# Block-sparse attention with a squared-ReLU layer on one core: key copies, v copies and order of the first chunk

## The chip, the cores and the metric

The kernel runs on one core of a Trainium2 chip. A core has a matrix engine (PE in the profile, with its weight loads as PEld), VectorE (DVE), ScalarE (ACT), GpSimd (POOL) and a queue engine (SP) that only starts transfers. Each engine works through its own list of instructions in order, and engines wait for each other by semaphores. The metric is the device time of one execution in microseconds (us); lower is better.

## The reference

```python
scores = scale * np.matmul(q, k.transpose(0, 1, 3, 2))
...
mask = np.abs(blk_i - blk_j) <= window
mask = mask | (blk_i == 0) | (blk_j == 0) | (blk_i == n_blocks - 1) | (blk_j == n_blocks - 1)
for qb in range(n_blocks):
    for kb in sampled_blocks[qb]:
        mask[qb * block:(qb + 1) * block, kb * block:(kb + 1) * block] = True
...
attn = attn / (np.sum(attn, axis=-1, keepdims=True) + 1e-09)
return np.matmul(attn, v).astype(np.float32)
...
h = np.maximum(x @ w_in, 0.0)
return (h * h @ w_out).astype(np.float32)
```

There are 4 batches of 8 heads, 768 positions and a head size of 64; 24 blocks of 32 positions. A block of queries attends to its neighbours, to the first and last block (the fixed blocks) and to 3 sampled blocks, whose indices are an input. The first and last block of queries attend to everything. The result, 3072 tokens of 512, goes through the dense layer 512 to 2048 to 512. All of it is float32.

## The kernel before

The queries of a batch make 6 tiles of 128 positions (4 blocks). Three tiles are a chunk; there are 8 chunks. The dense layer (`moe`) runs on one chunk while the attention of the next ones is woven into it. Before the first dense rows there is nothing to weave into, so the attention of chunk 0 runs alone, in a loop of its own near the end of the program.

**Units.** `Whole(b, pr)` handles the first and last block of queries for one pair of heads; `Half(b, t, u)` handles the other blocks of tile t for one half u of the heads (4 of 8). Both are generators: scores on PE, maxima on VectorE, exponentials on ScalarE (`exps`), transposes on PE (`turn`), copies out of PSUM (`copies`), the product with v on PE (`values`, tile `pv` or `pvg`), division by the sum on VectorE (`norm`). They yield after each step the number of steps to wait (`LAG_0`), and `Stream.step(now)` resumes them. `units(0)` gives the order: four Wholes, then six Halves, one every 5 steps (`STEP_0`). The order of the program is the order on each engine: it is written out by hand and nothing reorders it.

**Keys.** `load_keys` brings the keys of one half of the heads into a tile `kn` (24 blocks, 2 pairs of heads, 32 positions); POOL starts these two loads. For each tile of queries, `copy_keys` gathers on POOL what its 4 blocks need into `KG`: per half, the two fixed blocks for all four (`static_keys`, L297, 128x512) and then one copy per block and sample (L275, 128x64: two pairs of 32), whose source is addressed by a register. That is 24 small copies per tile (18 where a tile has only three blocks of its own). It yields after each block's three copies. Tiles 0 to 2 are copied before the loop; tiles 3 and 4 are put into `later` by the loop, and one yield of theirs is issued every second step (`KEYS_N`).

**v.** For each tile two tiles `V[k]` hold the rows of v that its blocks need: fixed rows, three window rows, three sampled rows. In chunk 0, tile 0's fixed rows come by DMA for one block and are copied by ScalarE to its other blocks (`copy_static`, L217); ScalarE also copies them for tiles 1 and 2, four copies of 64x1040, in steps 7 and on (`FIXED_0`). Tile 0's window rows come by DMA; those of tiles 1 and 2 are copied from `vn` with `copy_window` (L225, 32x260, twelve per tile and half): tile 1's first half and both halves of tile 2 on POOL, tile 1's second half on VectorE, one per step from step 22 (`MOVES_0`). The sampled rows come by DMA from SP (`load_sampled`, L323), one transfer per block and sample.

**Weights.** They arrive as 64-bit numbers. POOL starts the load of a block into `craw` (L782), ScalarE makes two parts of it (L798, L800), VectorE joins them (L809, L810), and the block of the first layer is split into a high and a low part: `WI` (ScalarE L816, POOL L817) or `wi` (ScalarE L842, POOL L845). `cut_next` moves this on by a stage. It is called five times before the loop, between POOL's key and v copies, then every 5 steps from step 35 (`CUT_0`), and inside the dense rows every 3 steps. The split of block 0 (L817) is issued at step 45, ahead of that step's load. The tiles `craw`, `wi` and others share one ring of 7 buffers.

**Dense rows.** `moe(0)` transposes the three tiles (`turn`), then for each of 16 weight blocks does `hidden` (12 matmuls into `ph`, L882: first with the high part, then the low part, then with the low part of x; then relu and square on ScalarE, L886 and L889) and, two blocks behind, `project` (L911). PE interleaves with this the scores of chunk 1.

Of the kernel before, what the change touches and what calls it, by code (L numbers as in the profile page):

```python
# [10 lines left out]
F32 = mybir.dt.float32  # L11
# [3 lines left out]
AF = mybir.ActivationFunctionType  # L15
# [8 lines left out]
BLK = 32  # L24
NBLK = S // BLK
NRAND = 3
P = 128
# [21 lines left out]
UC = 3  # L49
# [21 lines left out]
STEP_0 = 5  # L71
# [26 lines left out]
def tile_block_sparse_attention_moe(ctx: ExitStack, tc, kd, knd, qd, qgd, vd, vnd, samp, const, wcat, out):  # L98
# [9 lines left out]
    nc = tc.nc  # L108
    wide = wcat.dtype != F32

    one = ctx.enter_context(tc.tile_pool(name="one", bufs=1))
    rot = ctx.enter_context(tc.tile_pool(name="rot", bufs=2, reuse_waits="tile"))
# [12 lines left out]
    negative = one.tile([P, 1], F32, name="negative")  # L125
    nc.gpsimd.memset(negative, -SCALE)

    def indices():

        n = NBLK * NRAND  # L130
        si = rot.tile([1, 2 * n], I32, tag="r", name="si", bufs=2)
        nc.sync.dma_start(si, samp)
        rows = rot.tile([1, 6 * n], F32, tag="ct", name="rows", bufs=2)
        qb, s, m, d, keep, ne = (rows[:, i * n : (i + 1) * n] for i in range(6))
        nc.sync.dma_start(qb, const)
        nc.vector.tensor_copy(s, si.rearrange("p (r t) -> p r t", t=2)[:, :, 0])
        nc.vector.tensor_scalar(m, s, 0.5, None, op0=ALU.is_ge)
        nc.vector.scalar_tensor_tensor(m, s, NBLK - 1.5, m, op0=ALU.is_le, op1=ALU.mult)
        nc.vector.tensor_tensor(d, s, qb, op=ALU.subtract)
        nc.vector.tensor_tensor(d, d, d, op=ALU.mult)  # L140
        nc.vector.scalar_tensor_tensor(keep, d, 1.5, m, op0=ALU.is_ge, op1=ALU.mult)
        s3 = s.rearrange("p (b r) -> p b r", r=NRAND)
        k3 = keep.rearrange("p (b r) -> p b r", r=NRAND)
        ne = ne[:, :NBLK]
        for a, r in ((0, 1), (0, 2), (1, 2)):
            nc.vector.tensor_tensor(ne, s3[:, :, a], s3[:, :, r], op=ALU.not_equal)
            nc.vector.tensor_tensor(k3[:, :, r], k3[:, :, r], ne, op=ALU.mult)
        idx = one.tile([1, 2 * n], I32, name="idx")
        i4 = idx.rearrange("p (t i r) -> p t i r", i=2, r=NJ * NRAND)
        for i, x in enumerate((m, keep)):  # L150
            nc.vector.tensor_tensor(
                i4[:, :, i],
                x.rearrange("p (t r) -> p t r", t=NT),
                s.rearrange("p (t r) -> p t r", t=NT),
                op=ALU.mult,
            )
        return idx

    QG = one.tile([P, NPAIR, 2, BLK], F32, name="QG")
    V = {0: [one.tile([P, NJ, 2, HW // 2], F32, name=f"V{c}") for c in range(2)]}  # L160
    W1 = {f: one.tile([P, DM], F32, name=f"W1{f}") for f in SINGLE}
    KG = [one.tile([P, NJ, 2 + NRAND, NPAIR, BLK], F32, name=f"KG{i}") for i in range(2)]
# [4 lines left out]
    st = {}  # L167
# [3 lines left out]
    def load_whole(b, eng=nc.sync):  # L171

        eng.dma_start(QG.rearrange("p a b c -> p (a b c)"), qgd[b])

    def load_keys(b, u, eng=nc.sync):

        kn = rot.tile([P, NBLK, 2, BLK], F32, tag=f"kn{u}", name=f"kn{b}_{u}", bufs=1)
        eng.dma_start(kn.rearrange("p a b c -> p (a b c)"), knd[b, u])
        st["kn", b, u] = kn

    def values_of(k):

        return V[k if k < UC else 0]

# [3 lines left out]
    def halves(k, u):  # L188

        if k < UC:  # L190
            return slice(0, 2) if u == k // 2 else None
        return slice(u, u + 1)

    def columns(src, us):

        n = HW // 2
        return src[..., us.start * n : us.stop * n]

    def places(v, rows, js, us):

        return columns(v[rows, js].rearrange("p j u c -> p j (u c)"), us)

    def load_static(k, u, eng=nc.sync):
        us = halves(k, u)
        if us is None:
            return
        n = 1 if k == 0 else NJ
        src = columns(vd[order[k][0], V_STATIC * BLK :], us)
        src = src.unsqueeze(1).broadcast_to([2 * BLK, n, src.shape[-1]])
        eng.dma_start(places(values_of(k)[0], slice(0, 2 * BLK), slice(0, n), us), src)  # L210

    def copy_static(k, i, copy):

        us = slice(i, i + 1)
        src = places(V[0][0], slice(0, 2 * BLK), slice(0, 1), us)
        dst = places(V[k][0], slice(0, 2 * BLK), slice(1 if k == 0 else 0, NJ), us)
        copy(dst, src.broadcast_to(list(dst.shape)))  # L217

    def copy_window(k, i, j, n, copy):
# [4 lines left out]
        r = blk % NJ * BLK  # L224
        copy(V[k][1][(1 + n) * BLK : (2 + n) * BLK, j, i], st["vn", b, i][r : r + BLK, blk // NJ])  # L225

# [24 lines left out]
    def load_q(b, t, eng=nc.sync, own=None):  # L251
        q = (own or rot).tile([P, NJ, NPAIR, BLK], F32, tag="q", name=f"q{b}_{t}", bufs=1 if own else 2)
        n = NJ * NPAIR * BLK
        eng.dma_start(q.rearrange("p a b c -> p (a b c)"), qd[b, :, t * n : (t + 1) * n])
        st["q", b, t] = q
# [9 lines left out]
    def copy_keys(b, t, own=None):  # L265

        vals = sampled(t, 0, POOL)
        kg = keys_of(b, t, own)
        for u in range(2):
            if t < UC:  # L270
                static_keys(b, t, u, nc.gpsimd.tensor_copy)
            kn = st["kn", b, u]
            for j in sorted(groups(t)):
                for r in range(NRAND):
                    nc.gpsimd.tensor_copy(  # L275
                        kg[:, j, 2 + r, 2 * u : 2 * u + 2].unsqueeze(1), kn[:, bass.ds(vals[NRAND * j + r], 1)]
                    )
                yield

    later = []  # L280
# [12 lines left out]
    def static_keys(b, t, u, copy=nc.scalar.copy):  # L293

        src = st["kn", b, u][:, 0 : NBLK : NBLK - 1].rearrange("p i a c -> p i (a c)").unsqueeze(1)
        dst = st["kg", b, t][:, :, 0:2, 2 * u : 2 * u + 2].rearrange("p j i a c -> p j i (a c)")
        copy(dst, src.broadcast_to(list(dst.shape)))  # L297
# [13 lines left out]
    def load_sampled(k, u, eng, on):  # L311
        us = halves(k, u)
        if us is None:
            return
        b, t = order[k]
        VA, VB = values_of(k)
        vals = sampled(t, 1, on)
        v4 = columns(vd[b], us).rearrange("(a p) c -> p a c", p=BLK)
        for j in sorted(groups(t)):
            for r in range(NRAND):  # L320
                at = slice(0, BLK) if r == 2 else slice((2 + r) * BLK, (3 + r) * BLK)
                dst = places(VB if r == 2 else VA, at, slice(j, j + 1), us)
                eng.dma_start(dst, v4[:, bass.ds(vals[NRAND * j + r], 1)])  # L323
# [251 lines left out]
    class Whole:  # L575
# [32 lines left out]
        def scores(self):  # L608
# [4 lines left out]
            for g in range(NJ):  # L613
                kh, i = divmod(g, 2)
                for e in range(2):
                    r = slice(e * D, (e + 1) * D)
                    nc.tensor.matmul(  # L617
                        self.sg[e][g * BLK : (g + 1) * BLK, : self.n],
                        QG[r, pr, i],
                        kn[r, kh * NBLK // 2 : (kh + 1) * NBLK // 2, pr % 2, :],  # L620
# [98 lines left out]
    def units(c):  # L719

        halves = [Half(b, t, u) for b, t in order[c * UC : (c + 1) * UC] for u in range(2)]
        wholes = [] if c % 2 else [Whole(c // 2, pr) for pr in range(NPAIR)]
        if c == 0:
            return [(i * STEP_0, u) for i, u in enumerate(wholes + halves)]
        if c == 1:
            return [(i * STEP_1 + FIRST_1, u) for i, u in enumerate(halves)]
        at = begins(c - 1) - EARLY
        both = [(at + i * STEP, u) for i, u in enumerate(halves)]
        both += [(at + i * STEP + G_AT, u) for i, u in enumerate(wholes)]
        return sorted(both, key=lambda x: x[0])  # L730
# [250 lines left out]
    for k in range(1, UC):  # L981
        V[k] = [begin.tile([P, NJ, 2, HW // 2], F32, name=f"V{k}{c}") for c in range(2)]
    load_keys(0, 0, nc.gpsimd)
# [7 lines left out]
    load_q(0, 1)  # L991
    load_sampled(0, 0, nc.sync, SP)
    load_sampled(1, 0, nc.sync, SP)
    load_q(0, 2, own=begin)
    load_sampled(2, 1, nc.sync, SP)
    windows = {
        (k, u): [(copy_window, k, u, j, n) for j in range(NJ) for n in range(3)]
        for k in range(1, UC)
        for u in range(2)
    }  # L1000
    for k in range(2):
        deque(copy_keys(0, k), 0)
    for i in range(AHEAD + 1):
        if i == FIRST_LOADS:
            for f, *at in windows[1, 0]:
                f(*at, nc.gpsimd.tensor_copy)
        if i == SECOND_LOADS:
            deque(copy_keys(0, 2, begin), 0)
        if i == THIRD_LOADS:
            for f, *at in windows[2, 0] + windows[2, 1]:  # L1010
                f(*at, nc.gpsimd.tensor_copy)
        if i < AHEAD:
            cut_next()
    fixed = [(copy_static, k, i) for k in range(UC) for i in range(2)]
    moves = windows[1, 1]
    side = lambda name: ps_o.tile([P, 512], F32, tag="o", name=name)
    work = Stream()
    for at, u in units(0):
# [96 lines left out]
```

## Time and profile before

| | us |
|---|---|
| time, median of 3 runs | 748.9 (748.66 to 751.27) |
| the profiled execution | 750.76 |
| its span, first to last instruction | 749.0 |
| PE busy | 713.9 (95%) |
| DVE busy | 512.4 (68%) |
| ACT busy | 509.2 (68%) |
| POOL busy | 496.3 (66%) |

The page divides the span into 40 slices of 18.7 us and gives the busy share of each in tenths:

```profile
PE   4776999999999999999999999999999999999996
DVE  5985777757876775778877676678877677645432
ACT  4585786998876777579876777579876777622222
POOL 5997644237777466677867566667876566768783
```

A digit 9 is 90% or more. PE's first four slices, 75 us, are the attention of chunk 0 and the first dense rows; VectorE and POOL have their highest digits there. A timeline line reads: start, duration, engine, line of the program, operation, output<-inputs, shape, count, and in brackets the idle time before it with what ended it. Instructions on POOL overlap by some tens of nanoseconds, so the distance from start to start tells what one costs.

### The profile page before, as it was taken

How to read it: one execution, taken by the hardware profiler on the slowest of the kernel's cores; microseconds unless marked ns; L12 is line 12 of the kernel's file. 1: busy time of each engine (PE TensorE's matmuls, PEld its weight loads, DVE VectorE, ACT ScalarE, POOL GpSimd, SP SyncE). 2: the span in 40 equal slices, each digit the busy share in tenths (PEclk: the TensorE clock that was granted, in tenths of full speed). 3: DMA queues.
4: the chain of work that ended last, by engine and by line, in shares of the span. 5: the costliest groups of instructions: out<-in, count | busy, mean ns of one | idle time of the engine just before them, and what ended most of it. 6: DMA issues, size and time to landing. Idle time of an engine off the chain costs nothing.

```text
span 749.0 us, 25271 instructions
## 1 busy us (share of the span) xinstructions
PE 713.9 (95%) x9440; PEld 590.7 (79%) x9440; DVE 512.4 (68%) x992; ACT 509.2 (68%) x1121; POOL 496.3 (66%) x649
## 2 busy tenths in 40 slices
PE   4776999999999999999999999999999999999996
PEld 1565676668888888877888888877888888889895
DVE  5985777757876775778877676678877677645432
ACT  4585786998876777579876777579876777622222
POOL 5997644237777466677867566667876566768783
PEclk9998999999999999999999999999999999999999
DMA  8666789743443445544344344534344342101001
GB/s 273 199 173 196 230 238 311 202 126 98 121 104 101 113 107 164 157 99 122 97 125 111 80 132 131 182 92 142 86 129 108 86 132 52 33 2 42 1 1 43
DMA packets 84318, 92.49 MB, mean 123 GB/s; under 512 B 13507, under 2 KB 70596, under 8 KB 84196
## 3 DMA queue, kind: packets, MB, share of 16 engines
q1 hardware_dynamic: 78244, 68.03, 34.2%
q0 software_dynamic: 5664, 22.45, 9.3%
q8 instruction: 75, 1.23, 0.7%
q14 instruction: 47, 0.39, 0.2%
q10 hardware_dynamic: 288, 0.39, 0.1%
HBM read 84.53 MB, written 6.29 MB: 121 GB/s over the span
## 4 chain that ended last, share of the span: by engine, by line
PE 82%; POOL 4%; DVE 3%; issue 3%; DMA 3%; ACT 3%; POOLq 1%; SPq 0%; ACTq 0%
PE ph L882 34%; PE po L922 31%; PE s L401 6%; PE pv L496 5%; PE po L911 3%; POOL V L225 2%; POOL KG L275 2%; DMA KG<-in_k_dram 2%; PE pvg L685 1%; DMA V<-in_v_dram 1%; PE g L617 1%; DVE xl L872 1%; DVE WO L810 1%; ACT craw L800 0%; PE pv L511 0%
## 5 line engine op out<-in xcount | busy, mean ns | idle before, releaser
L446 ACT ACTIVATE pm<-p 32x256 f32<-32x256 f32 x528 | 219.3, 415 | 19.0 <-DVE p L421 11.3
L845 POOL TENSOR_TENSOR wo<-WO,wo 128x512 fp32r<-128x512 f32 x112 | 144.8, 1293 | 62.3 <-DVE wo L844 59.9
L882 PE MATMUL ph<-xh,wi 128*128 128x384 f32 x832 | 176.3, 348 | 7.4 <-POOL wi L845 5.3
L886 ACT ACTIVATE r<-ph 128x384 f32<-128x384 f32 x128 | 63.0, 492 | 168.3 <-PE ph L882 167.5
L845 POOL TENSOR_TENSOR wi<-W,wi 128x512 fp32r<-128x512 f32 x104 | 134.9, 1297 | 64.0 <-ACT wi L842 28.2
L922 PE MATMUL po<-wo,gh 128*128 128x512 f32 x672 | 176.0, 396 | 0.0
L901 POOL TENSOR_TENSOR gl<-gf,gh 128x384 fp32r<-128x384 f32 x112 | 113.8, 1016 | 85.3 <-DVE gf L898 70.3
L882 PEld LDWEIGHTS ph<-xh,wi 128*128 128x128 f32 x832 | 147.3, 188 | 28.5 <-issue 11.4
L898 DVE SCALAR_TENSOR_TENSOR gf<-ph,r 128x384 f32<-128x384 f32 x112 | 62.3, 556 | 146.8 <-ACT r L886 144.6
L922 PEld LDWEIGHTS po<-wo,gh 128*128 128x128 f32 x672 | 123.7, 188 | 24.4 <-issue 4.0
L922 PE MATMUL po<-wo,gl 128*128 128x512 f32 x336 | 98.5, 401 | 0.0
L882 PE MATMUL ph<-xl,wi 128*128 128x384 f32 x416 | 91.0, 341 | 0.0
L882 PEld LDWEIGHTS ph<-xl,wi 128*128 128x128 f32 x416 | 74.5, 189 | 2.0 <-issue 1.9
L922 PEld LDWEIGHTS po<-wo,gl 128*128 128x128 f32 x336 | 62.2, 189 | 16.9 <-issue 2.8
L844 DVE TENSOR_REDUCE wo<-WO 128x512 fp32r<-128x512 f32 x112 | 74.8, 668 | 0.0
L413 DVE TENSOR_REDUCE m<-s 128x2 f32<-128x512 f32 (+1 forms) x96 | 61.6, 683 | 12.2 <-PE s L401 12.0
L893 ACT ACTIVATE gh<-r 128x384 fp32r<-128x384 f32 x112 | 58.9, 526 | 10.0 <-ACT r L886 0.8
L844 DVE TENSOR_REDUCE wi<-W 128x512 fp32r<-128x512 f32 x91 | 61.0, 670 | 0.0
L401 PE MATMUL s<-KG,q 64*32 64x160 f32 x1408 | 48.2, 300 | 2.0 <-issue 1.1
L911 PE MATMUL po<-WO,gp 128*128 128x512 f32 x96 | 46.4, 618 | 0.0
L421 DVE TENSOR_TENSOR p<-s,m 128x512 f32<-128x512 f32 (+1 forms) x72 | 46.0, 679 | 0.0
L452 DVE STREAM_TRANSPOSE pT<-pm 128x1024 f32<-128x1024 f32 (+1 forms) x36 | 41.2, 1145 | 0.0
(95 smaller groups left out, 882.7 us busy)
## 6 DMA issues: line engine op xcount, KB each, us to landing
craw<-in_w_dram POOLq DMA_DIRECT2D x32, 512.0 KB, 5.2
V<-in_v_dram SPq DMA_DIRECT2D x462, 32.5 KB, 1.8
KG<-in_k_dram SPq DMA_DIRECT2D x198, 64.0 KB, 1.9
V<-in_v_dram SPq DMA_DIRECT2D x28, 390.0 KB, 4.1
q<-in_q_dram SPq DMA_DIRECT2D x24, 256.0 KB, 2.8
out_dram<-ot SPq DMA_DIRECT2D x22, 256.0 KB, 2.7
V<-in_v_dram SPq DMA_DIRECT2D x14, 292.5 KB, 4.2
vn<-in_vn_dram SPq DMA_DIRECT2D x5, 780.0 KB, 5.6
```

What stands on the lines that cost most here:

```text
L401: nc.tensor.matmul(self.sb[e][g * BLK : (g + 1) * BLK, i * NSLOT + a : i * NSLOT + z], q[r, j, pr, :], k, start=True, stop=True,)
L413: nc.vector.tensor_reduce(m[at, e], self.sb[e][at].rearrange("p (i c) -> p i c", i=2), axis=AX, op=ALU.max)
L446: nc.scalar.activation(p[a * BLK : (a + 1) * BLK, g], x[g * BLK : (g + 1) * BLK, :, a], AF.Exp, scale=SCALE)
L844: nc.vector.tensor_reduce(w[:, 0], src.unsqueeze(2), axis=AX, op=ALU.max)
L845: nc.gpsimd.tensor_tensor(w[:, 1], src, w[:, 0], op=ALU.subtract)
L882: nc.tensor.matmul(ph[:, :TOK], w, x, start=(i == 0), stop=(i == len(steps) - 1))
L886: nc.scalar.activation(r, ph[:, :TOK], AF.Relu)
L893: nc.scalar.activation(gh, r, AF.Square)
L898: nc.vector.scalar_tensor_tensor(gf, ph[:, :TOK], 0.0, r, op0=ALU.max, op1=ALU.mult)
L901: nc.gpsimd.tensor_tensor(gl, gf, gh, op=ALU.subtract)
L911: nc.tensor.matmul(acc[c][u], g[:, u * P : (u + 1) * P], WO[f], start=(f == 0), stop=(f == NF - 1))
L922: nc.tensor.matmul(acc[c][u], g[:, at], w[:, k], start=first, stop=(f == NF - 1 and g is gl))
```

## The change

Five things are changed, all for chunk 0.

- A one-element exponential is issued on ScalarE right after its operand `negative` is set.
- `kn` of both halves becomes one tile `KN` with the half as a dimension. `copy_keys` copies a sampled block for both halves in one instruction (128x128). For tile 0 it keeps the two passes, one per half. The other tiles have one pass, so half as many yields.
- The fixed rows of v for tiles 1 and 2 are loaded by DMA from SP, behind the sampled rows of tile 1; ScalarE's copies for these tiles are gone.
- The second half of tile 1's window rows is copied by POOL, ahead of tile 2's, and not by VectorE.
- `units(0)` puts the first Half behind the second Whole.

```diff
+    warm = one.tile([P, 1], F32, name="warm")
+    nc.scalar.activation(warm, negative, AF.Exp)
...
+    KN = one.tile([P, 2, NBLK, 2, BLK], F32, name="KN")
...
-        kn = rot.tile([P, NBLK, 2, BLK], F32, tag=f"kn{u}", name=f"kn{b}_{u}", bufs=1)
+        kn = KN[:, u]
...
-        for u in range(2):
+        for us in (slice(0, 1), slice(1, 2)) if t == 0 else (slice(0, 2),):
             if t < UC:
-                static_keys(b, t, u, nc.gpsimd.tensor_copy)
-            kn = st["kn", b, u]
+                for u in range(us.start, us.stop):
+                    static_keys(b, t, u, nc.gpsimd.tensor_copy)
             for j in sorted(groups(t)):
                 for r in range(NRAND):
-                    nc.gpsimd.tensor_copy(
-                        kg[:, j, 2 + r, 2 * u : 2 * u + 2].unsqueeze(1), kn[:, bass.ds(vals[NRAND * j + r], 1)]
-                    )
+                    to = kg[:, j, 2 + r].rearrange("p (u i) s -> p u (i s)", u=2)
+                    of = KN.rearrange("p u k i s -> p u k (i s)")
+                    nc.gpsimd.tensor_copy(to[:, us].unsqueeze(2), of[:, us, bass.ds(vals[NRAND * j + r], 1)])
                 yield
...
-            return [(i * STEP_0, u) for i, u in enumerate(wholes + halves)]
+            return [(i * STEP_0, u) for i, u in enumerate(wholes[:2] + halves[:1] + wholes[2:] + halves[1:])]
...
     load_sampled(1, 0, nc.sync, SP)
+    for k in range(1, UC):
+        load_static(k, k // 2)
     load_q(0, 2, own=begin)
...
         if i == THIRD_LOADS:
-            for f, *at in windows[2, 0] + windows[2, 1]:
+            for f, *at in windows[1, 1] + windows[2, 0] + windows[2, 1]:
                 f(*at, nc.gpsimd.tensor_copy)
...
-    fixed = [(copy_static, k, i) for k in range(UC) for i in range(2)]
-    moves = windows[1, 1]
+    fixed = [(copy_static, 0, i) for i in range(2)]
+    moves = []
```

## The prediction

> **What bounds the kernel now.** I read the head of the page first, then what the matrix engine waits for before 66 us and after 70 us, then the timelines of PE and POOL between 13 and 81 us.
>
> ```profile
> span 749.0 us, 25271 instructions
> PE ph L882 <- POOL wi L845: 5.3, 1, 5.3
> PE ph L882 <- DVE wi L844: 2.0, 2, 1.2
> ```
>
> The second line is the longest wait of PE between the attention of the first chunk and the dense rows; the third is the longest group of waits in all the time after 70 us. So PE sets the pace from 70 us on, and a gain must be made before that. The timeline of PE shows where:
>
> ```profile
> 51.19 1.38 PE L511 MATMUL pv<-V,pT 128*32 128x65 f32 x64 [0.92 <-ACT pT L485]
> 54.86 0.97 PE L882 MATMUL ph<-xh,WI 128*128 128x384 f32 x4 [0.82 <-ACT xh L871]
> 56.38 0.58 PE L401 MATMUL s<-KG,q 64*32 64x160 f32 x16
> 57.48 0.96 PE L882 MATMUL ph<-xh,WI 128*128 128x384 f32 x4 [0.51 <-POOL WI L817]
> 65.16 1.65 PE L882 MATMUL ph<-xh,wi 128*128 128x384 f32 x4 [5.32 <-POOL wi L845]
> 80.42 1.12 PE L511 MATMUL pv<-V,pT 128*32 128x65 f32 x64
> ```
>
> PE waits twice for POOL: 0.51 us for the low part of the first weight block (L817), then 5.32 us for that of the second (L845). POOL itself is never idle in between; it works through a queue:
>
> ```profile
> 13.90 1.65 POOL L275 COPY KG<-kn 128x64 f32 x9
> 15.49 0.61 POOL L297 COPY KG<-kn 128x512 f32<-128x512 f32 x1
> 16.05 2.18 POOL L275 COPY KG<-kn 128x64 f32 x12
> 20.85 1.05 POOL L782 DMA_DIRECT2D craw<-in_w_dram  x2
> 27.91 0.61 POOL L297 COPY KG<-kn 128x512 f32<-128x512 f32 x1
> 33.85 0.54 POOL L782 DMA_DIRECT2D craw<-in_w_dram  x1
> 34.44 12.16 POOL L225 COPY V<-vn 32x260 f32<-32x260 f32 x24
> 47.11 5.39 POOL L275 COPY KG<-kn 128x64 f32 x18
> 56.17 1.25 POOL L817 TENSOR_TENSOR WI<-ct,WI 128x512 fp32r<-128x512 f32 x1
> 57.38 0.58 POOL L782 DMA_DIRECT2D craw<-in_w_dram  x1
> 63.82 1.28 POOL L845 TENSOR_TENSOR wi<-W,wi 128x512 fp32r<-128x512 f32 x1
> ```
>
> Both waits end when POOL reaches an instruction that stands behind key copies. **POOL's queue is the bound of the first 65 us**, so the sum is made on it.
>
> **The change on POOL, step by step.** A merged key copy (128x128) is not in this trace. Nine copies of 64 elements fill 13.90 to 15.49, 0.177 us each; one of 512, read in eight runs of 64, fills 15.49 to 16.05, 0.56 us. So a further run of 64 costs (0.56-0.177)/7 = 0.054, and a merged copy 0.231 us. The bounds are 0.18 (a second run for nothing) and 0.355 (two old copies); I take 0.231, because the copy of 512 has the same runs.
>
> - Tile 1 ran from 15.49 to 20.85, 5.36 us: two fixed copies at 0.56 and 24 small ones. Now 2 x 0.56 + 12 x 0.231 = 3.89: -1.47.
> - Tile 2 ran from 27.91 to 33.85, 5.94 us. Now 3.89: -2.05; the copies that VectorE ran beside it are gone too.
> - Twelve copies of v move here, ahead of the 24 at 34.44. What one costs, and what VectorE's weight operations add, shows in the chain of work, copy by copy, with a row of VectorE's timeline below:
>
> ```profile
> 39.32 0.40 POOL V L225
> 39.78 0.79 POOL V L225
> 40.60 0.77 POOL V L225
> 39.59 0.70 DVE L809 SCALAR_TENSOR_TENSOR ct<-ct,craw 128x512 int32<-128x512 int32 x1
> ```
>
> Against a copy of 0.40, the two that start beside L809 and L810 take 0.79 and 0.77: such a pair costs POOL 0.76. Two pairs fell among the 24 copies (12.1 us), so one copy is (12.1-1.5)/24 = 0.44 and the twelve add +5.28.
> - Two more pairs fell on the 18 small copies at 47.11: 5.34-18 x 0.177 = 2.15. POOL now copies v until about 50 us and meets all four pairs there, at 0.76 each: -0.6.
> - Ahead of L817 stood 33 small copies of tiles 3 and 4. A tile now yields four times instead of eight, one yield for every second step, so tile 4 is through before the step that issues L817: 24 merged ones. 24 x 0.231 - 33 x 0.177: -0.3.
>
> L817 so starts 0.86 us later, at 57.03, ends near 58.3, and everything behind it is short: between 57.38 and 63.82 stood 15 small copies and three load issues. The copies are gone; the issues stay, 0.54 each. L845 starts at 58.3 + 1.6 = 59.9 instead of 63.82 and ends at 61.2. **PE's second block starts at 61.2 instead of 65.16: -3.9 us.**
>
> **What is late next.** ScalarE. Its timeline behind the first block:
>
> ```profile
> 59.17 0.49 ACT L886 ACTIVATE r<-ph 128x384 f32<-128x384 f32 x1 [3.85 <-PE ph L882]
> 64.70 1.54 ACT L460 ACTIVATE p<-s,m 128x256 f32<-128x256 f32 x4
> 68.13 0.49 ACT L886 ACTIVATE r<-ph 128x384 f32<-128x384 f32 x1 [1.89 <-PE ph L882]
> 73.66 0.61 ACT L816 CAST WI<-ct 128x512 fp32r<-128x512 f32 x1
> 75.20 0.49 ACT L886 ACTIVATE r<-ph 128x384 f32<-128x384 f32 x1 [0.93 <-PE ph L882]
> 77.37 0.56 ACT L485 COPY pT<-pt 128x512 f32<-128x512 f32 x1
> ```
>
> Take out its two waits for PE. From the first relu to the end of the exponentials it works 7.07 us (with a wait for VectorE), from the second relu to the end of L816 6.14, from the third to the end of the copy at 77.37 2.73: 15.94 in all. The first relu moves by the 0.86 of L817, to 60.03, so the copy ends at 75.97. The matmuls at 80.42 read it: they start at 76.0. PE would be there sooner (below), so ScalarE decides: **-4.4 us at 80.42**. From there PE has no gap longer than the waits shown, and I carry the 4.4 to the end.
>
> **The clock** belongs to it. Means by stretch (us; PE, PEld, DVE, ACT, POOL busy; PEclk; DMA share; GB/s):
>
> ```profile
> 10.00:12.00 2.00, 0.33 (x3) 0.31 (x3) 0.97 (x5) 1.99 (x4) 0.00 (x0) 1.00 1.02 332
> 12.00:14.00 2.00, 1.27 (x17) 0.54 (x19) 0.56 (x1) 2.00 (x4) 0.66 (x2) 0.75 1.04 330
> 64.00:66.00 2.00, 0.84 (x3) 0.84 (x4) 1.13 (x2) 2.00 (x6) 1.98 (x3) 0.55 0.73 188
> 70.00:72.00 2.00, 2.00 (x5) 0.72 (x3) 1.38 (x2) 0.46 (x2) 0.00 (x0) 0.74 0.87 342
> ```
>
> After the idle 5.32 us the granted clock is half from about 64.2 (a mean of 0.55 is 1.8 us of 2 at half) to 71.0 us (0.74 is 1.04 of 2), which costs PE (71.0-65.16)/2 = 2.9. From 65.16 to 80.42 PE thus has 15.26-2.9 = 12.3 us of work at full clock; from 61.2 it would be ready at 73.5, before ScalarE's 76.0. The new gap is shorter: the scores that end at 56.96 hang on the pv at 51.19, which then waits for POOL's last copy of v. POOL ends that at 33.85-3.5 (tiles 1, 2) + 0.6 + 36 x 0.44 + 4 x 0.76 = 49.8, so the scores end at 55.6 and PE is idle 2.7 us until 58.3. [...]
>
> **The parts that I cost at nothing**, since POOL covers them. VectorE loses twelve copies:
>
> ```profile
> L225 DVE COPY V<-vn x12: 285/292/695, 22.3 to 35.0; 32x260 f32<-32x260 f32 x12
> 30.00:35.00 5.00, 4.24 (x163) 3.37 (x153) 4.66 (x15) 2.42 (x6) 4.92 (x20) 1.00 0.62 173
> 9.65 1.28 ACT L641 ACT_TABLE_LOAD   x1 [9.65 <-DVE mg L634]
> ```
>
> VectorE is busy 4.66 us of 5 there, so at least 12 x 0.29 = 3.5 us less work there brings the attention's last pv from 51.19 towards 47.7, where POOL's 49.8 is later: about 2 us of this gain lie idle. The same holds for the table load (1.28 us off the first exponential) and for ScalarE's four copies of fixed blocks. The half tile moved up fills PE's wait for the second key half, but its pv must wait for the sampled rows of v that SP loads one by one, and whole tiles 2 and 3 queue behind it; the 2 us of cover hold that as well. If the cover were gone (POOL faster), each would count.
>
> The two DMAs go on SP's queue between the loads of tile 1 and q:
>
> ```profile
> 28.80 0.99 SPq L254 DMA_DIRECT2D q<-in_q_dram  x1
> 31.27 8.89 SPq L323 DMA_DIRECT2D V<-in_v_dram  x12
> V<-in_v_dram SPq DMA_DIRECT2D x1, 585.0 KB, 13.0
> ```
>
> Each carries 64 x 4 x 520 floats, 520 KB. Two issues at about half a us push the q load to 30 and the last sampled load of tile 2 from 40.2 to 41.2. The nearest landing is 13.0 us (585 KB, in the crowd at the start): lower bound of the harm 0, upper bound 28.8 + 13.0 = 41.8 for the pv of tile 1, which then runs 2 us late and is still covered. I take 0.
>
> **Sum.** 749.0 - 4.4 = 744.6 of span, 746.4 for the profiled execution of 750.76, which stands 1.9 above the median; against the median 748.9 that is **744.5 us**.
>
> **Rivals.**
> - *Half clock at the first block.* If PE's 2.7 us bring the gate down, the eight matmuls between 58.3 and the relu take twice their 1.7 us: the relu moves to 61.7, and 2.7 us are left: 746.2. For it: the fall at 12 to 14 us. Against: scores end only 2.7 us before.
> - *A merged copy costs as two (0.355).* POOL loses 48 x 0.124 = 6.0: L817 ends at 64.3, PE idles 8.7 us, the clock is surely half (+1.7). The matmuls at 80.42 start at 76.0 + 7.7 = 83.7: slower by 3.3, 752.2. The point at which nothing is left is 0.231 + 2.7/48 = 0.29 us a copy. Against it: the eight runs of the copy of 512.
> - *A merged copy costs 0.18.* POOL gains another 2.4; L817 ends at 55.9, hard behind the scores, with no gap: 742.1.
> - *The change does less than it says*: if the one key tile is tracked as a whole, the first copies and scores wait for the landing of its second half too. POOL's copies of the first half, now done before that, then stand in the queue like those of the second, which took 0.56 + 1.59 = 2.15 us up to 15.49; 4.4 - 2.15 are left: 746.7. Against it: at 54.86 PE reads one half of WI, while POOL has yet to write the other (only 57.48 waits for L817).
>
> **How the numbers follow.** Forecast 744.5: 0.48; half clock 0.20; two-for-one 0.13; 0.18 a copy 0.13; whole-tile wait 0.06. The range leaves out the two-for-one case and a little at the low end: 741.0 to 750.0. Half a per cent, 3.74 us (about what a measurement tells from no change), puts the border at 745.16, close above the forecast; I count 0.37 of its 0.48 below, with the 0.13 and 0.01 of the others: faster 0.51. Two-for-one lies at the upper border, half of it beyond: slower 0.09, with a little for a DMA that is late; same 0.40.
>
> **What would show it.** L275's copies on POOL at 0.23 apart; L817 starting near 57; no key copy between L817 and L845; L845 starting near 60; PE's wait there under 1 us; a granted clock of 1.0 from 58 to 71; PE then waiting for ScalarE's L485 before 76. L817 past 59, or the last pv waiting for V's DMA rather than POOL, would make me wrong.

## The result and the profile after

| | before | after |
|---|---|---|
| median of 7 runs each, us | 749.51 (746.57 to 753.12) | 745.61 (743.64 to 749.48) |
| ratio, 95% interval | | 0.9942 [0.9915, 0.9969] |
| profiled execution, us | 750.76 | 748.10 |
| its span, us | 749.0 | 746.3 |

The ratio is worth 4.3 us (the two medians are 3.9 apart), and the forecast was 4.4. The two profiled spans are only 2.7 us apart. In the first 66 us, PE's old waits for POOL are gone, and new ones stand elsewhere. This is the view of waits, after, from 0 to 66 us (who waited for whom: us in total, times, longest):

```profile
span 746.3 us, 25153 instructions
PE pv L515 <- issue: 5.8, 2, 4.6
PE pvg L689 <- issue: 3.1, 2, 1.8
POOL wi L849 <- ACT wi L846: 2.2, 1, 2.2
```

No line of PE waiting for POOL is left. Now POOL itself stands idle before L849 (L845 of before), because ScalarE brings its input late. Behind its start (6.3 us until the first keys land) the longest wait of PE is 4.6 us of "issue": no semaphore that the profile shows ended it. The timeline of POOL, after:

```profile
16.45 2.90 POOL L281 COPY KG<-KN 128x128 f32 x12
19.28 1.05 POOL L786 DMA_DIRECT2D craw<-in_w_dram  x2
30.65 16.69 POOL L229 COPY V<-vn 32x260 f32<-32x260 f32 x36
56.09 1.31 POOL L821 TENSOR_TENSOR WI<-ct,WI 128x512 fp32r<-128x512 f32 x1
57.32 1.62 POOL L786 DMA_DIRECT2D craw<-in_w_dram  x3
61.14 1.27 POOL L849 TENSOR_TENSOR wi<-W,wi 128x512 fp32r<-128x512 f32 x1 [2.21 <-ACT wi L846]
```

The merged copy takes (19.28 - 16.45)/12 = 0.236 us. L821 (L817 of before) starts at 56.09, and behind it stand only the three load issues. The timeline of PE, after:

```profile
34.16 0.87 PE L515 MATMUL pv<-V,pT 128*32 128x65 f32 x32
39.67 0.87 PE L515 MATMUL pv<-V,pT 128*32 128x65 f32 x16 [4.64 <-issue]
55.79 1.38 PE L515 MATMUL pv<-V,pT 128*32 128x65 f32 x64 [0.93 <-ACT pT L489]
64.15 1.57 PE L886 MATMUL ph<-xh,wi 128*128 128x384 f32 x8
75.34 1.98 PE L886 MATMUL ph<-xh,wi 128*128 128x384 f32 x8
77.55 1.58 PE L515 MATMUL pv<-V,pT 128*32 128x65 f32 x64 [0.23 <-issue]
```

PE stops in the middle of one product with v: 32 matmuls run, then nothing for 4.64 us, then the other 16 of the same group. Before, the same group stood at 34.17, and its break was 0.94 us, as the first of these two lines of PE's timeline before shows:

```profile
35.97 0.53 PE L511 MATMUL pv<-V,pT 128*32 128x65 f32 x15 [0.94 <-issue]
58.97 0.87 PE L882 MATMUL ph<-xh,wi 128*128 128x384 f32 x4
```

So the attention's last pv comes at 55.79, 4.6 us later than before (51.19). The second line concerns the second weight block. PE needs its high part first and then its low part, which L849 writes. Before, the four matmuls of the high part ran at 58.97, and the 65.16 of the prediction is the low part behind its wait. After, all eight run in one go from 64.15, and the low part, the fifth of them, starts near 64.9: only 0.3 us earlier. The pv of chunk 1 at 77.55 is 2.9 us earlier (80.42 before), and this reaches the end as 2.7 us of span. Between the low part and this pv lie 12.7 us instead of 15.3, mostly because the half clock that the prediction saw there from 64.2 to 71.0 no longer comes. What the stall leaves in the clock is in the windows of after (busy us of PE, PEld, DVE, ACT, POOL; granted clock; DMA share; GB/s):

```profile
36.00:40.00 4.00, 0.33 (x10) 0.33 (x12) 0.00 (x0) 0.37 (x1) 3.58 (x9) 0.89 0.80 250
40.00:44.00 4.00, 4.00 (x85) 3.16 (x79) 2.81 (x6) 2.12 (x5) 3.67 (x8) 0.50 0.42 97
44.00:48.00 4.00, 4.00 (x150) 3.46 (x136) 3.24 (x8) 2.93 (x7) 3.63 (x10) 0.75 0.84 251
```

From 36 to 40 PE works 0.33 us and VectorE nothing; only POOL works on. Then the granted clock is half: 0.89 is 0.9 us of 4 at half, 0.50 all of it, 0.75 is 2.0 us, together 6.9 us. It sets in at 39.1, while PE still stands. At the same place the DMA view shows slow landings. From 28 to 40 us, issues with KB each and median us to landing, first after, then before:

```profile
V<-in_v_dram SPq DMA_DIRECT2D x2, 520.0 KB, 7.1
craw<-in_w_dram POOLq DMA_DIRECT2D x1, 512.0 KB, 9.4
q<-in_q_dram SPq DMA_DIRECT2D x1, 256.0 KB, 8.8
```

```profile
craw<-in_w_dram POOLq DMA_DIRECT2D x1, 512.0 KB, 4.4
q<-in_q_dram SPq DMA_DIRECT2D x1, 256.0 KB, 4.2
```

With the two new loads of 520 KB in flight, a load of weights and one of q took about twice as long: 9.4 us against 4.4, and 8.8 against 4.2. The first lines of ScalarE's timeline, after, show the early table load:

```profile
0.75 1.28 ACT L129 ACT_TABLE_LOAD   x1 [0.75 <-PEq L1112]
9.63 1.05 ACT L645 ACTIVATE pg<-g,mg 128x384 f32<-128x384 f32 x2 [7.38 <-DVE mg L638]
```

The first exponential starts at 9.63 instead of 10.95. So the total is close to the forecast, while the way to it was in part another one.

### The profile page after: what moved, and what is told of

It is laid out like the page before. It is cut to its first block, busy times and chain, and to the rows that moved or that the text cites. A ratio compares the mean times of both kernels' runs of the same rounds, so it can differ in the third digit from the quotient of the medians.

```text
span 746.3 us, 25153 instructions
## 1 busy us (share of the span) xinstructions
PE 715.4 (96%) x9440; PEld 592.0 (79%) x9440; DVE 510.3 (68%) x980; ACT 505.6 (68%) x1118; POOL 490.6 (66%) x604
## 3 DMA queue, kind: packets, MB, share of 16 engines
q8 instruction: 75, 1.23, 0.7%
## 4 chain that ended last, share of the span: by engine, by line
PE 87%; DVE 4%; DMA 3%; ACT 3%; issue 2%; SPq 0%; ACTq 0%; POOL 0%; POOLq 0%; DVEq 0%
PE ph L886 34%; PE po L926 31%; PE s L405 7%; PE pv L500 5%; PE po L915 3%; PE pvg L689 2%; DMA V<-in_v_dram 2%; PE g L621 2%; PE pv L515 1%; PE pt L479 1%; DMA KG<-in_k_dram 1%; DVE xl L876 1%; DMA KN<-in_kn_dram 1%; DVE mg L634 1%; DVE W L813 0%
## 5 line engine op out<-in xcount | busy, mean ns | idle before, releaser
L849 POOL TENSOR_TENSOR wo<-WO,wo 128x512 fp32r<-128x512 f32 x112 | 144.9, 1294 | 61.3 <-DVE wo L848 57.1
L849 POOL TENSOR_TENSOR wi<-W,wi 128x512 fp32r<-128x512 f32 x104 | 135.2, 1300 | 63.9 <-ACT wi L846 28.0
L417 DVE TENSOR_REDUCE m<-s 128x2 f32<-128x512 f32 (+1 forms) x96 | 61.6, 682 | 15.3 <-PE s L405 15.3
L915 PE MATMUL po<-WO,gp 128*128 128x512 f32 x96 | 44.8, 601 | 0.0
```

Of the source, the lines that this page charges most:

```text
L417: nc.vector.tensor_reduce(m[at, e], self.sb[e][at].rearrange("p (i c) -> p i c", i=2), axis=AX, op=ALU.max)
L849: nc.gpsimd.tensor_tensor(w[:, 1], src, w[:, 0], op=ALU.subtract)
L915: nc.tensor.matmul(acc[c][u], g[:, u * P : (u + 1) * P], WO[f], start=(f == 0), stop=(f == NF - 1))
```

## The experiments

The theory after reading the two traces: the two loads of v's fixed blocks crowd the DMA engines, PE's next instructions come late through the same engines, and this stall with its half clock takes back part of what POOL gained. The rivals: the half tile moved up makes the stall (its pv is the one that breaks); or the stall is chance. Each kernel was timed side by side with the kernel before, in series of several kernels, and each ratio is to the kernel before of its own series. The parts are called merge (key copies), loads (fixed blocks by DMA), windows (v copies on POOL), order (half tile moved up) and table (early exponential).

| parts | median us | ratio to before [95%] | profiled span us | longest issue wait of a pv or pvg, us |
|---|---|---|---|---|
| all five | 745.61 | 0.9942 [0.9915, 0.9969] | 746.3 | 4.6 |
| all five, again | 745.57 | 0.9932 [0.9904, 0.9960] | 744.5 | 4.4 |
| without loads | 745.74 | 0.9934 [0.9909, 0.9959] | 742.6 | 2.1 |
| without loads, again | 745.70 | 0.9931 [0.9909, 0.9954] | 741.7 | 1.7 |
| without order | 747.60 | 0.9959 [0.9934, 0.9983] | 746.1 | 4.6 |
| without windows | 747.42 | 0.9961 [0.9936, 0.9985] | 745.3 | 3.3 |
| loads alone | 750.72 | 1.0007 [0.9986, 1.0027] | 750.0 | 5.5 |
| all five, loads twice | 752.10 | 1.0021 [0.9997, 1.0045] | 752.3 | 3.2 |
| merge alone | 748.17 | 0.9966 [0.9942, 0.9989] | 743.1 | 0.5 |
| merge, order, table | 743.33 | 0.9906 [0.9873, 0.9938] | 742.4 | 1.2 |
| the same, again | 744.58 | 0.9918 [0.9886, 0.9950] | 742.7 | 1.2 |
| merge, windows, table | 745.52 | 0.9940 [0.9917, 0.9963] | 744.6 | 1.3 |
| merge, windows, order | 747.20 | 0.9957 [0.9936, 0.9978] | 744.0 | 1.5 |

**Without the loads.**

```diff
-    for k in range(1, UC):
-        load_static(k, k // 2)
...
-    fixed = [(copy_static, 0, i) for i in range(2)]
+    fixed = [(copy_static, k, i) for k in range(UC) for i in range(2)]
```

> The changed kernel with tile 1's and tile 2's fixed rows of v copied by ScalarE again, without the two 520 KB loads. Theory A (the loads crowd the DMA engines, so PE's next 16 KB of instructions lands late and PE stands 4.64 us inside the pv of tile 0's second half): that idle time falls to 0.9 to 1.3 us, as before the change, no half clock between 39 and 46 us, the last pv of the chunk starts near 50 us instead of 55.8, the dense rows' second block near 61; ratio to the kernel before 0.988 to 0.991. Theory B (PE stands there because the half tile put first changes when PE asks for instructions; the loads are innocent): 4 us or more stay, ratio 0.993 or more, since ScalarE's copies come back on top.

The timeline of PE without the loads:

```profile
36.86 0.53 PE L515 MATMUL pv<-V,pT 128*32 128x65 f32 x15 [0.53 <-issue]
58.72 0.98 PE L886 MATMUL ph<-xh,WI 128*128 128x384 f32 x4 [0.88 <-POOL WI L821]
61.86 0.97 PE L886 MATMUL ph<-xh,wi 128*128 128x384 f32 x4 [0.75 <-POOL wi L849]
74.64 1.60 PE L515 MATMUL pv<-V,pT 128*32 128x65 f32 x64 [0.22 <-issue]
```

The stall at this pv is 0.53 us instead of 4.64, the attention's last pv starts at 51.29, and now PE waits for POOL as the prediction had it. The pv of chunk 1 starts 2.9 us earlier than with the loads, the span is 3.7 us shorter. The median is not: 0.9934 against 0.9942.

The traces also have a DMA queue of the kind "instruction". This is its line on the page of the changed kernel (packets, MB, share), then the line of the DMA view from 37.1 to 38.2 us with the loads, then from 34.5 to 35.61 us without them:

```profile
q8 instruction: 75, 1.23, 0.7%
```

```profile
q8 instruction: 1, 0.02, 6.0%
```

```profile
q8 instruction: 1, 0.02, 6.1%
```

By this line a packet holds 16 KB (1.23 MB in 75), and the 75 come to one for about 252 of PE's 9440 matmuls and 9440 weight loads. With the loads, the view from 30.1 to 37.1 us has no such packet; the next one runs from 37.1 to 38.2, and PE goes on at 39.67, 1.5 us behind its end. Without the loads it runs from 34.5 to 35.6, and PE goes on at 36.86, 1.3 us behind. In the trace after, all four issue waits of a pv or pvg over 1 us (1.75, 1.30, 4.64 and 1.15 us, up to 26.96, 31.73, 39.67 and 50.06) end 1.5 to 1.7 us behind such a packet; in the trace before, the two longest of a pv (0.94 us up to 35.97, 1.21 us up to 45.47) end 1.4 us behind one. From this it is inferred that PE stood until its instructions had come, and that with the loads they came late. No view shows what a packet carries, nor whether it waits behind the bulk data or is asked for late.

**The old order, loads kept.**

```diff
-            return [(i * STEP_0, u) for i, u in enumerate(wholes[:2] + halves[:1] + wholes[2:] + halves[1:])]
+            return [(i * STEP_0, u) for i, u in enumerate(wholes + halves)]
```

> The changed kernel with the old order, four whole tiles and then the halves. Theory A: the two loads are still there and PE still stands 3.5 to 5 us within a pv between 33 and 41 us; ratio 0.993 to 0.998. Theory B: the idle time falls to about 1 us and the ratio to 0.991 or less.

PE's timeline with the old order:

```profile
39.73 0.86 PE L515 MATMUL pv<-V,pT 128*32 128x65 f32 x16 [4.63 <-issue]
```

The stall is the same to 0.01 us, so the order isn't its cause.

**The loads alone, and the loads twice.** The first is the kernel before with the two loads in place of ScalarE's copies; the second is the changed kernel with each load issued twice.

```diff
+    for k in range(1, UC):
+        load_static(k, k // 2)
...
-    fixed = [(copy_static, k, i) for k in range(UC) for i in range(2)]
+    fixed = [(copy_static, 0, i) for i in range(2)]
```

> The kernel before with only the two loads of fixed rows in place of ScalarE's four copies. Theory A: PE stands 3 us or more, marked as issue, within a pv between 33 and 42 us (0.94 before), and the kernel is slower by 1 to 4 us, ratio 1.001 to 1.005, unless POOL's queue covers it. Theory B: no such idle time, ratio 0.998 to 1.000.

```diff
-    for k in range(1, UC):
+    for k in (1, 2, 1, 2):
         load_static(k, k // 2)
```

> The changed kernel with the two 520 KB loads of fixed rows started twice, the second time with the same rows into the same places. Theory A: the idle time of 4.64 us grows by about the time of the added megabyte, 3 to 5 us, to 7 to 10 us, and the time by 2 to 5 us: ratio 0.997 to 1.003. Theory B: it stays at 4 to 5 us, ratio 0.994 to 0.996.

PE's timeline, first with the loads alone, then with the loads twice:

```profile
36.12 1.08 PE L511 MATMUL pv<-V,pT 128*32 128x65 f32 x23 [5.54 <-issue]
```

```profile
27.54 1.13 PE L689 MATMUL pvg<-vn,pTg 128*32 128x65 f32 x33 [2.66 <-issue]
39.39 0.54 PE L515 MATMUL pv<-V,pT 128*32 128x65 f32 x16 [3.20 <-issue]
```

The loads bring the stall into the kernel before, though at another pv. There it costs next to nothing (1.0007): presumably POOL's slow queue would have made PE wait there anyway. The low part of PE's second block starts near 66.1, 0.9 us later than before. With twice the loads the whole gain is gone: 1.0021 [0.9997, 1.0045] against 0.9942 [0.9915, 0.9969]. But the stall didn't grow to the 7 to 10 us that the theory expected: two of 2.66 and 3.20 stand there. The longest wait of PE behind its start is another one, for the load of q:

```profile
46.95 0.58 PE L405 MATMUL s<-KN,q 64*32 64x96 f32 x16 [5.29 <-DMA q<-in_q_dram]
```

So this run shows that more loads cost more, but not through the instructions alone.

**The merge alone.** Loads, windows, order and table as before.

> The kernel before with nothing but the one key tile and the merged key copies. Theory C (the merge carries the gain): POOL loses 3.8 us ahead of the low part of the first weight block and 8.6 us ahead of that of the second; PE's chain stays, its last pv near 51 us, so the second block of the dense rows starts near 60 us with no half clock after it; ratio 0.989 to 0.993. Theory D (the gain needs the other parts too): the attention's chain stays late and half of the gain is missing, ratio 0.995 to 1.000.

It gives 0.9966, with an interval below 1. PE's second block starts at 59.66, its low part near 60.4, 4.8 us earlier than before and without a wait for POOL, and the pv of chunk 1 at 73.12. So the profile goes as theory C said, but the ratio lies in the range of theory D.

**Merge, order and table.** ScalarE copies the fixed blocks, VectorE the windows.

```diff
-            for f, *at in windows[1, 1] + windows[2, 0] + windows[2, 1]:
+            for f, *at in windows[2, 0] + windows[2, 1]:
...
-    fixed = [(copy_static, 0, i) for i in range(2)]
-    moves = []
+    fixed = [(copy_static, k, i) for k in range(UC) for i in range(2)]
+    moves = windows[1, 1]
```

> The merged key copies, the half tile put earlier and the early exponential, with VectorE's twelve v copies and ScalarE's fixed rows as before the change. Theory C: as good as the merge alone within 0.002. Theory D: better by 1 to 3 us than the merge alone, because the first exponential and the half tile bring PE's chain forward while POOL has 5.3 us less to do than in the changed kernel; ratio 0.986 to 0.990.

This is the lowest median of all, 743.33, about 2.3 us under the changed kernel. It is also 4.8 us under the merge alone, which stood beside it: order and table together, with the windows off POOL, bring 0.9966 [0.9942, 0.9989] to 0.9906 [0.9873, 0.9938]. No wait of PE for POOL is left and, in this execution, no half clock from 16 to 64 us (windows, columns as above):

```profile
16.00:40.00 24.00, 17.50 (x553) 12.29 (x551) 22.60 (x64) 13.65 (x30) 22.56 (x63) 1.00 0.79 218
40.00:64.00 24.00, 19.02 (x458) 15.45 (x449) 19.07 (x37) 18.12 (x38) 17.31 (x40) 1.00 0.64 188
```

In the second profile of this kernel a half clock does come between 26 and 34 us (means of 0.73 and 0.85 over 26 to 30 and 30 to 34), with a span only 0.3 us longer.

**Without order, and without table, both without the loads.**

> The changed kernel without the two loads (ScalarE copies the fixed rows) and with the old order of units. If the half tile put earlier is worth something once the loads are gone: 1 to 2 us slower than without the loads alone, ratio 0.994 to 0.997. If POOL's queue covers it, as predicted: the same, 0.992 to 0.994, with POOL's first weight block near 57 us in both.

> The changed kernel without the two loads and without the early exponential, so that the table is loaded ahead of the first real one again. If POOL's queue covers the 1.28 us, as predicted: the same time as with it, ratio 0.992 to 0.994. If PE's chain sets the end: about 1 us slower, ratio 0.994 to 0.996.

The old order gives 0.9940 beside 0.9934: no difference that can be told. Without the early table load it is 0.9957. The intervals overlap. PE's timeline shows what goes with it, by the same six transposes twice, first without the early table load, then with it:

```profile
11.73 0.93 PE L666 MATMUL ptg<-ident,pg 128*128 128x128 f32 x6 [2.56 <-ACT pg L642]
16.38 1.54 PE L666 MATMUL ptg<-ident,pg 128*128 128x128 f32 x6
```

```profile
10.38 1.51 PE L669 MATMUL ptg<-ident,pg 128*128 128x128 f32 x6 [1.28 <-ACT pg L645]
15.10 0.88 PE L669 MATMUL ptg<-ident,pg 128*128 128x128 f32 x6
```

With it PE's first transposes start 1.35 us earlier. But six of them take about 0.9 us at a granted clock of 1.00 (0.87 at 21.71, after) and 1.5 at half (the 1.54 at 16.38 above, where the clock from 16 to 20 is 0.51): without the early load they are fast first and slow later, with it slow first and fast later. The windows must be read with care here, first without, then with the early load:

```profile
12.00:16.00 4.00, 3.23 (x94) 2.40 (x96) 2.34 (x4) 4.00 (x8) 2.80 (x12) 0.63 1.01 336
```

```profile
10.00:12.00 2.00, 1.62 (x15) 1.32 (x20) 1.02 (x6) 2.00 (x4) 0.00 (x0) 1.00 1.02 336
```

The second row has a clock of 1.00 while the transposes in it take 1.51 us. So in this first stretch a clock of 1.00 stands beside a length like that at half, and the lengths are what is compared here. The kernel before, also without the early load, is fast in both places (0.93 at 11.67, 0.90 at 16.31), with a clock of 0.50 from 13 to 16 between them. That the early table load spares a half clock is thus not shown.

**Four kernels side by side.** Because the median of the kernel without the loads didn't follow its profile, it and the best one were run again beside the changed kernel, with a kernel that keeps the loads and gives the windows back to VectorE.

> The changed kernel once more, beside the next three on one chip. Theory (the loads cost what the stall shows, 2 to 4 us): this kernel comes out 2 to 4 us above the same kernel without the two loads. Rival (the profile caught an execution with an unusually long stall, and the usual one is short): the two agree within 1 us, and this profile shows a stall inside tile 0's pv of under 2 us.

> The changed kernel without the two loads (ScalarE copies the fixed blocks), once more. Theory: 2 to 4 us below the changed kernel of the same call, the stall inside tile 0's pv under 1 us. Rival: within 1 us of it.

> Merged key copies, the half tile moved up and the early table load; fixed blocks on ScalarE and the windows on VectorE as before. If its lead is real, 1.5 to 3 us below the changed kernel of the same call (ratio to the kernel before 0.987 to 0.993). If it was chance, within 1 us of the changed kernel.

> The changed kernel with the windows of tile 1's second half back on VectorE; the loads stay. If POOL's twelve extra copies cost something even beside the stall, 0.5 to 2 us below the changed kernel, with L821 starting near 52. If the stall covers them, within 0.5 us of the changed kernel; the stall of 3 to 5 us and the half clock stay in either case.

PE's timeline of the changed kernel, then of the one without the loads:

```profile
40.21 0.87 PE L515 MATMUL pv<-V,pT 128*32 128x65 f32 x16 [4.37 <-issue]
76.60 1.58 PE L515 MATMUL pv<-V,pT 128*32 128x65 f32 x64 [0.24 <-issue]
```

```profile
45.12 0.77 PE L515 MATMUL pv<-V,pT 128*32 128x65 f32 x36 [1.49 <-issue]
74.14 1.45 PE L515 MATMUL pv<-V,pT 128*32 128x65 f32 x64 [0.25 <-issue]
```

The profiles repeat: the stall of 4.4 us with the loads, none over 1.7 us without, 2.5 us between the two at chunk 1 and 2.8 us of span. The medians repeat too: 745.57 and 745.70, no difference. So both expectations of the theory on the medians failed, and the rival's on the profile failed as well. The profiled executions with the loads lay 2.5 and 0.7 us above the medians of their kernel, those without them 1.4 and 2.3 us below: this makes the 3 us of difference between the profiles. The best kernel lies 1.0 us below the changed one here, less than the 1.5 expected. With the loads kept and the windows on VectorE it is 0.9961, not better; L821 then starts at 51.91, but POOL waits 5.51 us for ScalarE before L849, so POOL's time is not what is missing there.

What holds over all of them: the six profiles with the loads have an issue wait of 3.2 us or more, the seven without have none over 2.1. That the loads cause the stall is shown. What it costs over many executions is shown only in part: the four pairs that differ by the loads alone (all five and without them; without order; without windows and the best; loads alone and before) differ in the ratio by 0.0008, 0.0019, 0.0055 and 0.0007, always against the loads, some 0.5 to 4 us; in the last series the first and the third pair differ by 0.0001 and 0.0043. There the kernels of a pair stood side by side. Drawing their times again at random puts the difference of the medians, 2.8 us for the third pair, between 0.6 and 4.7 us in 95% of the draws, and that of the first between -2.1 and 1.8. So the loads cost something where VectorE copies the windows, and nothing that can be told in the changed kernel, where POOL copies them. Executions of one kernel scatter by up to 11 us (all five, again: 741.81 to 752.49); of the merge alone (743.56 to 751.60) the profiled one lay 3.3 us under the median. So a difference of 3 us between two single profiles doesn't yet say what the medians will do. Whether the executions without a profile have the same stall can't be seen and stays open.

## Why the prediction was right, and where it was not

**The merged copy: right.** 0.231 us was forecast, 0.236 measured. The rivals of 0.355 and 0.18 fall. The wait for the whole key tile falls too: after, the first scores started at 6.25 us, and POOL waited for the second half until 13.18.

**POOL's queue: right, and a little early.** L817 (now L821) was forecast at 57.03 and started at 56.09, or 57.39 without the loads. Without the loads the last copy of v ended at 49.2, near the forecast of 49.8. In the changed kernel it ended at 47.3: with VectorE idle (0.00 from 36 to 40) fewer of its weight pairs seem to have fallen on those copies, and more on the key copies behind, which took 0.28 and 0.32 us each.

**"PE's second block starts at 61.2": wrong in the changed kernel.** The 61.2 is the low part, which started near 64.9, and L849 started at 61.14 instead of 59.9, held by ScalarE. Without the loads L849 started at 60.24 and the low part at 61.86. There the forecast holds within 0.7 us, with waits for POOL under 1 us as said.

**The step that failed: "The two DMAs ... I take 0".** The harm was looked for where the data is used, and there it was small: the pv of tile 1 has no wait for them. It came by another way that the bounds didn't cover: PE stood for 4.64 us, by the inference above because its own instructions were late, with half a clock for 6.9 us. In the profile that is 2.9 us at the pv of chunk 1 (77.55 against 74.64).

**The half clock: the rival was right that it comes, wrong in the place.** It was priced for a gap of 2.7 us before the first block at 55.6 to 58.3. It came at 39.1, 4.1 us into the gap of 4.64 us. The sum took those 2.7 us of idle PE as without effect on the clock, and no run shows that. After, PE's longest gap between 55 and 64 us was 1.07 us, and the clock stayed at 1.00 there. What the traces have is this. Before, in the gap of 5.32 us, the clock fell at 64.2, 4.4 us into it, and was half for 6.8 us. Also before, it was half from 13.0 to 16.4, where PE's longest gap since its first matmul was the 2.56 us up to 11.67. After, a gap of 1.75 us up to 26.96 left it at 1.00 (24 to 36). What 2.7 us do is left open by this. Another fall, in the last section, came behind a gap of 2.56 us too.

**"ScalarE decides" at 76.0: too long.** From the first relu to the end of the copy 15.94 us were counted. Two waits for VectorE were left in, as this part of ScalarE's timeline of before shows:

```profile
62.97 0.62 ACT L842 CAST wi<-W 128x512 fp32r<-128x512 f32 x1 [1.56 <-DVE WO L810]
71.92 0.62 ACT L842 CAST wi<-W 128x512 fp32r<-128x512 f32 x1 [1.54 <-DVE WO L810]
```

With ScalarE later or in step, VectorE has its part done: after, ScalarE has no wait over 0.2 us from the first relu (64.35) to the copy (76.53 to 77.09). The copy ends 12.7 us behind the start of the relu, 3.2 less than counted, about the two waits together. Moreover PE, not ScalarE, decides: the pv comes 0.23 us behind the ph of 75.34, and 12.7 us behind the low part; without the loads it is 12.8, with the merge alone 12.7. The prediction had this path with 12.3 us, ready at 73.5, and let ScalarE's 76.0 decide.

**The sum.** The pv of chunk 1 was forecast at 76.0. Without the loads it came 1.4 us earlier, because the chain through ScalarE was counted too long; the loads, taken at nothing, put it 2.9 us later again, 1.6 behind the forecast. The two errors have opposite signs: span 746.3 against 744.6 forecast, median 745.61 against 744.5. That the total came so close is partly luck. Without the loads the profiled spans are 742.6 and 741.7.

**"The table load at nothing"** may be wrong by 1 to 2 us (0.9957 against 0.9934 and 0.9931), not resolved. **The order** at nothing: 0.0006 without the loads and 0.0017 with them, not resolved. With the windows off POOL, order and table together are worth 0.0060 (merge alone against merge, order, table; 0.0048 against the second measurement of the latter): they count once POOL no longer covers them, as the prediction said. **The windows on POOL**: with the loads 0.9961 without the part against 0.9942 and 0.9932 with it; without the loads 0.9906 and 0.9918 against 0.9934 and 0.9931. The sign turns, and no pair is clear of its intervals. The best reading is that the merge is about half of the gain (0.0034 of 0.0058 to 0.0068), and that the version with merge, order and early table load is not shown to be slower than the changed kernel; its medians are 1.0 and 2.3 us lower, which isn't resolved, with two parts less.

## What to carry to other kernels

Here two loads of 520 KB, issued in the midst of short work, showed in the profile not only where their data is used: PE stood for 4.64 us (0.53 without them), and a load of weights took 9.4 us (4.4 before). So look at which other traffic is in flight at that moment, instructions among it, before a load is costed at nothing. When a chain is shifted, take its waits apart by what ended them: here ScalarE's two for VectorE, 1.56 and 1.54 us, left none over 0.2 us when ScalarE came later. And before believing 3 us between two single profiles, look at the spread of the medians: here a stall that every profile with the loads showed was worth 3 us in the changed kernel's profiles and nothing that could be told in its medians.

## What the hardware showed that was not expected

PE stood still for 3.2 to 5.5 us in the middle of a group of matmuls, with no semaphore of the profile open, in the six profiles with some 1 MB of loads (2 MB in one) put in flight; in the seven without them its longest such wait was 0.5 to 2.1 us. PE's weight loads stopped for about as long (after):

```profile
PEld pv L515 <- issue: 6.4, 3, 4.8
```

Here a packet of 16 KB on the instruction queue ended 1.5 us before PE went on.

The granted clock fell also behind shorter gaps: without the early table load it was half from about 13 us (means of 0.63 from 12 to 16 and 0.51 from 16 to 20), where PE's longest gap since its first matmul was the 2.56 us up to 11.73. And POOL's copy was cheap in width: one of 128 elements out of two runs took 0.236 us, two of 64 took 0.354.
